# A recurrence and a gated MLP on one core: the order of the operations is read from a stored table instead of planned while building

## The chip, the core and the metric

The kernel runs on one NeuronCore of a Trainium2 chip. The metric is device microseconds of one execution; the time of a kernel is the median over its runs.

Five engines are named as in the profile: PE multiplies matrices, DVE does elementwise and scan work, ACT evaluates functions and copies out of PSUM, POOL does masks and some elementwise work, SP issues all of this kernel's DMAs. Each engine works through its own list of instructions strictly in the order in which the program was built. An instruction whose inputs or buffers are not ready holds up everything behind it on its engine.

## The reference

Per batch and head (4 x 8) a 40x40 state is carried over 768 tokens; the 32 outputs of a token are then joined to a row of 320 numbers, which goes through an MLP without a nonlinearity other than one product.

```python
for t in range(S):                                   # S = 768
    y[:, :, t] = einsum('bhd,bhde->bhe', r[t], state)
    Sa = einsum('bhde,bhe->bhd', state, a[t])
    state = state * w[t][:, :, None, :] - einsum('bhd,bhe->bhde', Sa, b[t]) + einsum('bhd,bhe->bhde', v[t], k[t])
x = y.transpose(0, 2, 1, 3).reshape(B * S, H * D)    # 3072 x 320
out = ((x @ w1) * (x @ w2) @ w3) @ w_out             # d_ff = 1024
```

## The kernel before

The 768 tokens are cut into 12 chunks of 64, and the 32 heads into 2 groups of 8 pairs. What is serial inside a chunk becomes matrix work, and only the state goes from chunk to chunk. For chunk `c` and group `g`:

- `load` fetches the gates and keys (`fm`) and the `a` vectors (`lh`) by SP.
- `scale` makes running products of the gates by a scan on DVE (L436, L441), their inverses on ACT (L445, L448) and DVE (L457, L461), and scales `lh` (L453) and the keys in `fm` (L465), each on DVE or POOL by the chunk.
- `causal` multiplies them on PE (L490); ACT copies the result to `JP` and back to `lh`, POOL masks it (L508).
- `solve` inverts the triangular systems of all 16 pairs of a chunk on DVE alone: a transpose of `JP` into `ab` (L522, its first operation), 36 small products and sums, and two transposes into `TDX` (L597, L600). Each step reads what the one ahead of it wrote.
- `join` completes the inverse on PE (L623, L630).
- `pairs` (L667) and `tokens` (L694) prepare operands on PE.
- `rec` is the recurrence: PE (L718, L725, L733, L745, L778) alternates with ACT copies and four masked copies on DVE (L738), then the new state (L771) and the output `y` (L790) on DVE.
- `gather` moves `y` by 12 DMAs (L800), and `mlp` multiplies the 256 tokens of the chunk by the weights: `xs` is split into a high and a low part (ACT L825, DVE L828), 128 matmuls (L842), the product on DVE (L856), its low part on POOL or DVE (L859), and 48 matmuls (L868).

Ahead of the first `mlp` the weights must be read: `weights` brings them as 64-bit numbers in 31 pieces, and `convert` turns each into fp32 by three DVE operations (L333, L337, L341, each reading what the last wrote) and two on ACT. W3 is first multiplied by the output weights on PE (L404, `product`).

None of these functions emits an instruction at once. Each calls `op(engine, cost, due, fn, r=..., w=...)`, which notes an operation with what it reads and writes. The operations that need a buffer of a pool (`slot`; `bank` is PSUM, 6 of them) name it. After all 2970 operations are noted, `Order.place` plans them: from costs, latencies and due times in the table `P` it simulates the engines, picks the next operation of each and a buffer for it, and the operations are emitted in the order of their planned starts. The instructions of each engine are then tied to that order. The semaphore waits follow from what each one reads and writes.

Of the kernel before, what the change touches and what calls it, by code (L numbers as in the profile page):

```python
# [1 line left out]

# [15 lines left out]
B, H, S, D = 4, 8, 768, 40  # L18
# [15 lines left out]
LAT = dict(pe=0.33, act=0.09, dve=0.09, pool=0.1, sp=2.4, nil=0.0)  # L34
# [4 lines left out]
MODE = {"mlp": 0, "128": 0, "c40t": 0, "c64": 1, "c40": 1, "q64": 2, "32": 3}  # L39
DRAIN, LEAD = 0.1, {"mlp": 0.104, "c40t": 0.02, "32": 0.0}  # L40
# [3 lines left out]
         ga=21.36, ml=83.8, kp=5.81, mt=26.61, mg=18.52, sl=0.56, kw=2.39)  # L44

# [3 lines left out]
class Slot:  # L49


    def __init__(self, order, pool):
        self.order, self.pool, self.at, self.left, self.since, self.until = order, pool, None, 0, 0.0, 0.0
        if order.direct:
            self.at = order.turn[pool] = (order.turn.get(pool, -1) + 1) % SLOTS[pool]
# [6 lines left out]
class Order:  # L62
# [33 lines left out]
    def place(self):  # L96
        ops = self.ops
        for o in ops:
            o["users"], o["wait"] = [], len(o["deps"])
        for o in ops:  # L100
            for d in o["deps"]:
                ops[d]["users"].append(o)
        free = {p: dict.fromkeys(range(n), 0.0) for p, n in SLOTS.items()}
        ready = {e: [] for e in LAT}
        clock, last, lock, dma = {**dict.fromkeys(LAT, 0.0), "pool": 8.0, "dve": 4.0, "sp": 1.0}, None, {"dve": 0.0, "pool": 0.0}, 0.0
        for o in ops:
            o["ready"] = 0.0
            if not o["wait"]:
                ready[o["eng"]].append(o)

        def begin(o):

            t, left = max(o["ready"], clock[o["eng"]]), {}
            for s in o["slots"]:
                if s.at is None:
                    n = left[s.pool] = left.get(s.pool, 0) + 1
                    if len(free[s.pool]) < n:
                        return None
                    t = max(t, sorted(free[s.pool].values())[n - 1])
                else:  # L120
                    t = max(t, s.since)
            if o["two"]:
                t = max(t, lock["pool" if o["eng"] == "dve" else "dve"])
            return t

        uses = {p: {o["eng"] for o in ops for s in o["slots"] if s.pool == p} for p in SLOTS}
        placed, cand, spare = [], {}, {}

        def choice(e, starts):
            if not starts:  # L130
                return None
            first = min(t for t, _ in starts)
            if e != "pe":
                return first, min((o for t, o in starts if t <= first + 1e-9), key=lambda o: (o["due"], o["n"]))
            return min(((t, o) for t, o in starts if t <= first + P["sl"]),
                       key=lambda x: (x[1]["due"] - P["kp"] * (MODE[x[1]["kind"]] == MODE.get(last)) + P["kw"] * (x[0] - first), x[1]["n"]))

        while len(placed) < len(ops):
            best = None
            for e in LAT:  # L140
                if e not in cand:

                    starts, short = [], 1e9
                    for o in ready[e]:
                        t = begin(o)
                        if t is not None:
                            starts.append((t, o))
                        elif e == "pe" and any(s.pool == "bank" and s.at is None for s in o["slots"]):
                            short = min(short, o["due"] + P["mg"])
                    some = [x for x in starts if x[1]["due"] < short or not any(s.at is None for s in x[1]["slots"])]  # L150
                    spare[e] = len(some) < len(starts)
                    cand[e] = choice(e, some)
                if cand[e] and (best is None or cand[e][0] < best[0]):
                    best = cand[e]
            if best is None and any(spare.values()):
                e = "pe"
                best = choice(e, [(t, o) for o in ready[e] if (t := begin(o)) is not None])
            if best is None:
                raise ValueError(f"stuck after {len(placed)} of {len(ops)}")
            t, o = best  # L160
            e = o["eng"]
            ready[e].remove(o)
            stale = {e, *(("dve", "pool") if o["two"] else ())}
            cost = o["cost"]
            if e == "pe":
                if MODE[o["kind"]] != MODE.get(last):
                    cost += DRAIN + LEAD.get(o["kind"], 0.05)
                last = o["kind"]
            for s in o["slots"]:
                if s.at is None:  # L170
                    stale |= uses[s.pool]
                    s.at = min(free[s.pool], key=lambda i: (free[s.pool][i], i))
                    s.since = free[s.pool].pop(s.at)
# [924 lines left out]
```

## Time and profile before

| what | value |
|---|---|
| median of 3 runs | 678.53 us (677.45 to 679.85) |
| span of the profiled execution | 676.2 us |
| PE busy | 577.7 us |
| DVE busy | 551.4 us |
| ACT busy | 431.8 us |
| POOL busy | 211.9 us |

The profiled execution is one run of the same program; its span is counted from its first to its last instruction, and the median of the runs is 2.3 us above it. Busy time counts an engine's working instructions; an engine that waits is not busy. A matmul's end is modelled, so matmuls that follow each other closely overlap in the records. In the rows, `<-` names what ended an idle stretch.

### The profile page before, as it was taken

What the parts mean: (1) busy time and instruction counts of PE and PEld (TensorE: products, weight loads), DVE (VectorE), ACT (ScalarE), POOL (GpSimd) and SP (SyncE); (2) the same over time, 40 slices, a digit from 0 to 9 for tenths busy, and PEclk for the clock granted to TensorE, in tenths of its full rate; (3) what the DMA queues carried; (4) which work ended last, traced back from release to release, by engine and by line L of the source; (5) the groups of instructions that cost most, each with busy time, mean ns of one, the idle gap of its engine ahead of it and who ended that gap; (6) DMA issues with size and microseconds to landing.
All of it is one profiled execution on the core that took longest, in us unless ns stands there. A gap on an engine that the chain in (4) does not pass through costs nothing.

```text
span 676.2 us, 22337 instructions
## 1 busy us (share of the span) xinstructions
PE 577.7 (85%) x9458; PEld 515.3 (76%) x9458; DVE 551.4 (82%) x987; ACT 431.8 (64%) x927; POOL 211.9 (31%) x188
## 2 busy tenths in 40 slices
PE   1422996768799999898999989899999989999996
PEld 1321664556788999788989878789888889898996
DVE  7999999999999799798799798898987997914310
ACT  2886756686776865846837849559578477473321
POOL 4462005233521205505206316245044171120011
PEclk9999997978989999899999999999999999999999
DMA  7954564444214234034133143150341431110101
GB/s 187 245 148 139 169 159 126 132 124 92 60 31 105 69 88 102 14 94 104 33 94 79 32 98 74 42 147 16 83 111 38 99 72 32 45 32 12 34 21 24
DMA packets 61090, 57.56 MB, mean 85 GB/s; under 512 B 29560, under 2 KB 52600, under 8 KB 60984
## 3 DMA queue, kind: packets, MB, share of 16 engines
q1 hardware_dynamic: 60984, 56.07, 32.7%
q8 instruction: 76, 1.25, 0.8%
q14 instruction: 30, 0.25, 0.1%
HBM read 47.40 MB, written 3.93 MB: 76 GB/s over the span
## 4 chain that ended last, share of the span: by engine, by line
DVE 47%; PE 32%; ACT 8%; issue 6%; DMA 4%; POOL 1%; DVEq 0%; SPq 0%; POOLq 0%
PE bank L842 14%; DVE tmp L548 9%; DVE xu L738 6%; PE bank L868 5%; DMA fm<-in_fmx_dram 4%; DVE ab L552 3%; DVE mf L337 3%; ACT JP L212 3%; DVE Tp L552 3%; PE bank L745 2%; DVE fm L441 2%; DVE ab L522 2%; PE bank L725 2%; PE bank L490 2%; DVE w3f L341 2%
## 5 line engine op out<-in xcount | busy, mean ns | idle before, releaser
L842 PE MATMUL bank<-xs,W 128*128 128x256 f32 x1536 | 204.8, 289 | 0.7 <-DVE xs L828 0.7
L842 PEld LDWEIGHTS bank<-xs,W 128*128 128x128 f32 x1536 | 190.3, 193 | 5.8 <-DVE xs L828 0.9
L677 POOL TENSOR_SCALAR_AFFINE_SELECT xu<-xu 64x512 f32<-64x512 f32 x48 | 46.0, 958 | 187.9 <-ACT xu L212 172.1
L212 ACT ACTIVATE xu<-bank 64x256 f32<-64x256 f32 (+2 forms) x184 | 72.6, 437 | 39.4 <-PE bank L718 32.2
L859 POOL TENSOR_TENSOR gl<-ga,gh 128x512 fp32r<-128x512 f32 x32 | 41.0, 1283 | 109.8 <-ACT gh L212 109.8
L212 ACT ACTIVATE JP<-bank 32x512 f32<-32x512 f32 x120 | 60.5, 504 | 22.6 <-PE bank L490 20.7
L490 PE MATMUL bank<-lh,fm 40*64 40x64 f32 x1536 | 32.7, 236 | 45.0 <-POOL fm L465 23.3
L738 DVE TENSOR_TENSOR xu<-bank,mask_h 64x416 f32<-64x416 f32 x96 | 56.3, 587 | 14.0 <-PE bank L733 12.0
L490 PEld LDWEIGHTS bank<-lh,fm 40*64 40x64 f32 x1536 | 29.5, 149 | 49.4 <-POOL fm L465 25.9
L508 POOL TENSOR_SCALAR_AFFINE_SELECT lh<-lh 64x512 f32<-64x512 f32 x48 | 41.0, 853 | 76.8 <-ACT lh L212 73.9
L856 DVE TENSOR_TENSOR ga<-bank,ga 128x512 f32<-128x512 f32 x48 | 32.8, 683 | 39.1 <-PE bank L842 30.3
L868 PE MATMUL bank<-W3h,gh 128*128 128x320 f32 x192 | 63.1, 329 | 1.1 <-DVE xu L738 1.1
L868 PE MATMUL bank<-W3l,gh 128*128 128x320 f32 x192 | 59.2, 309 | 0.0
L868 PE MATMUL bank<-W3h,gl 128*128 128x320 f32 x192 | 59.2, 308 | 0.0
L404 PE MATMUL bank<-wof,w3f 128*128 128x320 f32 x128 | 41.7, 479 | 16.7 <-DVE w3f L341 16.7
L745 PE MATMUL bank<-xu,bk 128*40 128x104 f32 (+1 forms) x768 | 47.5, 262 | 5.9 <-DVE xu L738 5.8
L212 ACT ACTIVATE gh<-ga 128x512 fp32r<-128x512 f32 x48 | 30.3, 631 | 34.6 <-DVE ga L856 34.2
L725 PE MATMUL bank<-xu,lh 128*64 128x104 f32 (+2 forms) x768 | 43.4, 266 | 9.5 <-ACT xu L212 5.8
L453 POOL TENSOR_TENSOR lh<-lh,fm 104x1024 f32<-104x1024 f32 x16 | 35.4, 2216 | 48.4 <-DVE fm L441 22.3
L745 PEld LDWEIGHTS bank<-xu,bk 128*40 128x40 f32 (+1 forms) x768 | 37.5, 120 | 14.7 <-DVE xu L738 12.1
L725 PEld LDWEIGHTS bank<-xu,lh 128*64 128x64 f32 (+2 forms) x768 | 37.6, 144 | 14.2 <-ACT xu L212 6.9
L404 PEld LDWEIGHTS bank<-wof,w3f 128*128 128x128 f32 x128 | 25.8, 210 | 28.7 <-issue 14.3
(99 smaller groups left out, 1190.9 us busy)
## 6 DMA issues: line engine op xcount, KB each, us to landing
fm<-in_fmx_dram SPq DMA_DIRECT2D x24, 627.2 KB
raw<-in_w3t_dram SPq DMA_DIRECT2D x16, 512.0 KB
rv<-in_rv_dram SPq DMA_DIRECT2D x48, 160.0 KB
raw<-in_w_dram SPq DMA_DIRECT2D x8, 512.0 KB
lh<-in_fma_dram SPq DMA_DIRECT2D x48, 80.0 KB
xu<-in_vt_dram SPq DMA_DIRECT2D x48, 80.0 KB
out_dram<-o SPq DMA_DIRECT2D x48, 80.0 KB
xr<-y SPq DMA_DIRECT2D x72, 40.0 KB
```

What stands on the lines that cost most here:

```text
L212: act.activation(out_, in_, AF.Copy, scale=scale)
L404: pe.matmul(out=pt.t[:, 0:DM], lhsT=w[:, j], rhs=wof[:, j], start=(j == 0), stop=(j == NJ - 1))
L490: pe.matmul(out=bank(ab)[64 * x:64 * x + 64, p], lhsT=X[r, p, x], rhs=lh.t[r, ab, p], start=True, stop=True)
L508: pool.affine_select(out=lh.t[q, ab], in_=lh.t[q, ab], pattern=[[0, NP], [1, C]], compare_op=ALU.is_gt, fill=0.0, base=0, channel_multipli ...
L548: dve.tensor_tensor(out=scratch(*shape), in0=x().to_broadcast([128, *shape]), in1=y().to_broadcast([128, *shape]), op=ALU.mult)
L677: op("pool", 0.67, due + 2, lambda q=q, ab=ab: pool.affine_select(out=xu.t[q, ab, :, 0:C], in_=xu.t[q, ab, :, 0:C], pattern=[[0, NP], [1, ...
L725: pe.matmul(out=view(hp[h])[64 * ab:64 * ab + 64, u], lhsT=lh.t[k, ab, HP * h + u], rhs=xu.t[k, ab, HP * h + u], start=True, stop=True)
L738: dve.tensor_tensor(out=xu.t[64 * ab:64 * ab + 64, ab, k:NP:2], in0=view(us[ab])[r], in1=mask_h[r].unsqueeze(1).to_broadcast([64, HP, N]), ...
L745: pe.matmul(out=q(r, p), lhsT=bk.t[:, p, r], rhs=xu.t[:, ab, p], start=(c == 0), stop=True, skip_group_check=True)
L842: pe.matmul(out=pt.t[:, TOK * x:TOK * x + TOK], lhsT=WT[k][:, cs], rhs=xs.t[:, z], start=(n == 0), stop=(n == 7))
L859: both(ON["gl"][c % NCH], 1.3, 0.69, t + 1, lambda e, a=a, j=j: e.tensor_tensor(out=gl.t[:, j:j + 2], in0=a.t, in1=gh.t[:, j:j + 2], op=AL ...
L868: pe.matmul(out=pt.t[:, 0:DM], lhsT=l.t[:, j, ts], rhs=W3[r][:, j], start=(j == 0 and n == 0), stop=(j == NJ - 1 and n == 2))
```

## The change

`place` no longer plans. It decodes a string of numbers, `PLAN`: for each place in the program the operation that stands there, and for each buffer wanted the number that it gets. The same 2970 operations are emitted with the same costs and functions; the assertions only check that the order keeps every dependence. Two names, `turn` and `turns`, keep the weight pieces' loads and their first conversion steps in the order of the pieces.

```diff
-LAT = dict(pe=0.33, act=0.09, dve=0.09, pool=0.1, sp=2.4, nil=0.0)
...
+PLAN = """
+c-n<n2XvKH);;IG_tHo}iVluttf+_}NEc1$f+z_fN)-h~K%|!#0;JFhRX|Wj5kyoV1f(UQNdnRtz!4Rc@n;+r0Z9TO<(@P9do3^g|5|_6%6Gr-)^pF@d!K
...
     def place(self):
-        ops = self.ops
+        ops, n = self.ops, len(self.ops)
+        code = array("h", zlib.decompress(base64.b85decode("".join(PLAN.split()))))
+        turns, at = list(accumulate(code[:n])), iter(code[n:])
+        assert sorted(turns) == list(range(n))
         for o in ops:
...
-        while len(placed) < len(ops):
-            best = None
-            for e in LAT:
...
-        self.placed = sorted(placed, key=lambda o: (o["start"], o["n"]))
-        return self.placed
+        done, holder = set(), {}
+        placed = [ops[i] for i in turns]
+        for o in placed:
+            assert o["deps"] <= done
...
+        return placed
...
-        op("sp", 0.35, due - 8, f1, w=[raw], dma=2.5)
+        op("sp", 0.35, due - 8, f1, w=[raw, "turn"], dma=2.5)
...
-        op("dve", 0.42, due, f4, r=[raw], w=[mf], two=True)
+        op("dve", 0.42, due, f4, r=[raw], w=[mf, "turns"], two=True)
```

In the changed file a line of the functions above has a number that is 24 lower (L828 is L804 there). On all engines the order moves; three places are shown.

The first place is DVE near its start, where the first two pieces of the weights (`raw_139`, `raw_140`) are converted. Before:

```order
L333 TENSOR_SCALAR mf_145<-raw_139 128x512
L337 SCALAR_TENSOR_TENSOR mf_145<-raw_139,mf_145 128x512
L341 SCALAR_TENSOR_TENSOR mf_145<-raw_139,mf_145 128x512
L453 TENSOR_TENSOR lh_98<-lh_98,fm_94 104x1024
L333 TENSOR_SCALAR mf_146<-raw_140 128x512
L337 SCALAR_TENSOR_TENSOR mf_146<-raw_140,mf_146 128x512
L341 SCALAR_TENSOR_TENSOR mf_146<-raw_140,mf_146 128x512
```

Of the change, the same two pieces:

```order
L309 TENSOR_SCALAR mf_145<-raw_139 128x512
L441 TENSOR_TENSOR fm_93<-fm_93,gi_100 104x1024
L313 SCALAR_TENSOR_TENSOR mf_145<-raw_139,mf_145 128x512
L309 TENSOR_SCALAR mf_146<-raw_140 128x512
L317 SCALAR_TENSOR_TENSOR mf_145<-raw_139,mf_145 128x512
L313 SCALAR_TENSOR_TENSOR mf_146<-raw_140,mf_146 128x512
L417 SCALAR_TENSOR_TENSOR fm_95<-fm_95,first 104x520
L317 SCALAR_TENSOR_TENSOR mf_146<-raw_140,mf_146 128x512
```

The three steps of a piece stood next to each other, each reading the one ahead; now another piece or another chunk's scaling stands between them.

The second place is DVE just ahead of the first `mlp`, whose low part `xs` is written by L828 (`xu_106`, `st_110`, `y_111` from `fm_95` belong to `rec` of chunk 1, group 1; `fm_94` here to `scale` of chunk 3; `ab` to the solve of chunk 2). Before:

```order
L436 TENSOR_SCALAR fm_94,stats<-fm_94 104x520
L738 TENSOR_TENSOR xu_106<-bank_131,mask_h 64x4x104
L738 TENSOR_TENSOR xu_106<-bank_130,mask_h 64x4x104
...
L548 TENSOR_TENSOR tmp<-Tp,ab 128x512
L552 TENSOR_REDUCE ab<-tmp 128x16x4
L771 TENSOR_TENSOR st_110<-bank_134,fm_95 104x160
L790 TENSOR_TENSOR y_111<-bank_134,fm_95 104x4x64
...
L441 SCALAR_TENSOR_TENSOR fm_94<-fm_94,first 104x520
L453 TENSOR_TENSOR lh_98<-lh_98,fm_94 104x1024
L828 TENSOR_TENSOR xs_1519<-xr_112,xs_1519 128x768
```

Of the change:

```order
L524 TENSOR_TENSOR tmp<-Tp,ab 128x1024
L747 TENSOR_TENSOR st_110<-bank_131,fm_94 104x160
L766 TENSOR_TENSOR y_111<-bank_131,fm_94 104x4x64
L528 TENSOR_REDUCE ab<-tmp 128x16x4
L747 TENSOR_TENSOR st_110<-bank_134,fm_94 104x160
L766 TENSOR_TENSOR y_111<-bank_134,fm_94 104x4x64
L804 TENSOR_TENSOR xs_1410<-xr_112,xs_1410 128x768
L524 TENSOR_TENSOR tmp<-ab,DG 128x512
L528 TENSOR_REDUCE Tp<-tmp 128x8x8
```

The eight DVE operations of chunk 1, group 1 and three of chunk 3's scaling now stand behind the first `xs`; two long steps of the solve of chunk 2 stand ahead of it.

The third place is DVE where the solve of chunk 8 begins with the transpose of `JP_113` (`fm_93` is chunk 8's second group). Before:

```order
L457 TENSOR_TENSOR gt_101<-fm_93,gi_100 104x512
L461 SCALAR_TENSOR_TENSOR gi_100<-gt_101,gi_100 104x512
L465 TENSOR_TENSOR fm_93<-fm_93,gi_100 104x1024
L856 TENSOR_TENSOR ga_1520<-bank_134,ga_1520 128x512
L522 STREAM_TRANSPOSE ab<-JP_113 128x1024
```

Of the change:

```order
L441 TENSOR_TENSOR fm_93<-fm_93,gi_100 104x1024
L528 TENSOR_REDUCE R_128<-tmp 128x8x8
L568 TENSOR_TENSOR ab<-R_128,ab 128x8x8
L524 TENSOR_TENSOR tmp<-ab,DG 128x512
L528 TENSOR_REDUCE Tp<-tmp 128x8x8
L573 STREAM_TRANSPOSE TDX_102<-Tp 128x32x16
L576 STREAM_TRANSPOSE TDX_102<-TDX_102 128x512
L498 STREAM_TRANSPOSE ab<-JP_113 128x1024
```

Between the scaling of the keys and the transpose stood one operation of 128x512; now the last six steps of the solve of chunk 7 stand there.

## Rows read from the trace of the kernel before

**Rows 1.** The page: span, busy time, 40 slices, engines of the chain.

```profile
span 676.2 us, 22337 instructions
...
PE 577.7 (85%) x9458; PEld 515.3 (76%) x9458; DVE 551.4 (82%) x987; ACT 431.8 (64%) x927; POOL 211.9 (31%) x188
...
PE   1422996768799999898999989899999989999996
...
DVE  7999999999999799798799798898987997914310
...
DVE 47%; PE 32%; ACT 8%; issue 6%; DMA 4%; POOL 1%; DVEq 0%; SPq 0%; POOLq 0%
```

**Rows 2.** Windows: us, busy us of five engines, PE clock, DMA share, GB/s.

```profile
0.00:170.54 170.54, 100.61 (x1489) 75.66 (x1489) 158.98 (x287) 116.37 (x277) 58.93 (x62) 0.94 0.57 152
170.54:670.00 499.46, 476.95 (x7969) 439.69 (x7969) 392.31 (x699) 314.96 (x651) 152.95 (x126) 0.99 0.26 63
670.00:676.20 6.20, 0.10 (x2) 0.00 (x0) 0.15 (x1) 0.44 (x1) 0.00 (x0) 0.79 0.20 39
```

**Rows 3.** Timeline of DVE ahead of the first MLP: start, us, instruction.

```profile
161.28 0.70 DVE L436 TENSOR_SCALAR_CACHE_REDUCE fm<-fm 104x520 f32<-104x520 f32 x1 [0.26 <-DMA fm<-in_fmx_dram]
...
164.38 0.69 DVE L548 TENSOR_TENSOR tmp<-Tp,ab 128x512 f32<-128x512 f32 x1
165.10 0.69 DVE L552 TENSOR_REDUCE ab<-tmp 128x64 f32<-128x512 f32 x1
...
167.13 1.23 DVE L441 TENSOR_TENSOR_SCAN fm<-fm,first 104x520 f32<-104x520 f32 x1
168.39 1.23 DVE L453 TENSOR_TENSOR lh<-lh,fm 104x1024 f32<-104x1024 f32 x1
169.53 0.95 DVE L828 TENSOR_TENSOR xs<-xr,xs 128x768 fp32r<-128x768 f32 x1
```

**Rows 4.** Timeline of PE, same place.

```profile
170.54 1.68 PE L842 MATMUL bank<-xs,W 128*128 128x256 f32 x12 [0.70 <-DVE xs L828]
```

**Rows 5.** Who DVE waited for, 10 to 170 us: total, times, longest.

```profile
DVE fm L436 <- DMA fm<-in_fmx_dram: 1.9, 3, 1.4
```

**Rows 6.** Groups by line and shape: busy, mean ns.

```profile
L552 DVE TENSOR_REDUCE ab<-tmp 128x64 f32<-128x1024 f32 x12 | 14.7, 1222 | 0.2
L548 DVE TENSOR_TENSOR tmp<-Tp,ab 128x1024 f32<-128x1024 f32 x12 | 14.6, 1218 | 0.3
```

**Rows 7.** Window, 157.55 to 169.48 us.

```profile
157.55:169.48 11.93, 9.98 (x153) 7.88 (x153) 11.10 (x21) 9.46 (x21) 6.37 (x6) 0.86 0.44 95
```

**Rows 8.** Who PE waited for, from the first MLP matmul on.

```profile
PE bank L490 <- POOL fm L465: 6.7, 4, 2.7
PE bank L623 <- DVE TDX L600: 2.1, 2, 1.1
...
PE bank L490 <- issue: 1.9, 3, 1.4
```

**Rows 9.** Who DVE waited for, 170.6 to 592 us.

```profile
DVE ab L522 <- ACT JP L212: 23.4, 8, 3.9
```

**Rows 10.** Timeline of DVE, start of the solve of chunk 8.

```profile
419.27 2.19 DVE L465 TENSOR_TENSOR fm<-fm,gi 104x1024 f32<-104x1024 f32 x1
...
424.97 2.02 DVE L522 STREAM_TRANSPOSE ab<-JP 128x1024 f32<-128x1024 f32 x1 [2.54 <-ACT JP L212]
```

**Rows 11.** Timeline of SP, the first loads.

```profile
0.82 0.46 SPq L424 DMA_DIRECT2D fm<-in_fmx_dram  x1
2.04 0.66 SPq L427 DMA_DIRECT2D lh<-in_fma_dram  x2
```

**Rows 12.** Window, the first 25 us.

```profile
0.00:25.00 25.00, 7.13 (x144) 6.31 (x144) 20.61 (x27) 11.03 (x23) 11.75 (x25) 1.00 0.84 213
```

**Rows 13.** Timeline of DVE, end of the last solve.

```profile
592.84 0.71 DVE L600 STREAM_TRANSPOSE TDX<-TDX 128x512 f32<-128x512 f32 x1
```

**Rows 14.** Timeline of PE, the last join.

```profile
596.31 1.20 PE L623 MATMUL bank<-TDX,JP 32*32 32x32 f32 x64
```

More of the change, by code (lines that the diff above doesn't have):

```diff
@@ L1 @@
+import base64
+import zlib
+from array import array
 from contextlib import ExitStack
+from itertools import accumulate
 import concourse.bass as bass
@@ L46 @@
+4&uh+w~m4*VM07+{MH&jzADe{4&o}*s(`Jo;4a*iuoJ2mo)BDfkd5vj0xSH>!PNu4GJY0NCA53|^SOf_b5-&Y2QePXxC(?+oFMu4XZ${Mg(!n3hy!=XUVJ
+C$4q*@nacV+V@C5Dk1UXn4e^g1ODt7D%u_~Y~uAomU&ZGj{fwe;QDm0Ez5EmvGS6nwmql!~=hj6Dd+R5)D<JVPpCA&Ge6BFXY0LI*vG%?^6Pe{ZF*yr+d{
+AT+q6sSVOTtN=HLOg0hkngU9O;_+#Js~Ru)XB$qSCBpb1^6}XS^
+"""
 ON = dict(ws="p", lh="pdpddppdpppp", xs="dpppdpdpdddp", gl="pdpdppppdpdp")
@@ L52, in __init__ @@
     def __init__(self, order, pool):
-        self.order, self.pool, self.at, self.left, self.since, self.until = order, pool, None, 0, 0.0, 0.0
+        self.order, self.pool, self.at, self.left = order, pool, None, 0
         if order.direct:
@@ L96, in place @@
     def place(self):
-        ops = self.ops
+        ops, n = self.ops, len(self.ops)
+        code = array("h", zlib.decompress(base64.b85decode("".join(PLAN.split()))))
+        turns, at = list(accumulate(code[:n])), iter(code[n:])
+        assert sorted(turns) == list(range(n))
         for o in ops:
[L99 to L113, printed above, removed]
             for s in o["slots"]:
                 if s.at is None:
[L116 to L136, printed above, removed]
@@ L138, in place @@
-        while len(placed) < len(ops):
-            best = None
-            for e in LAT:
[L141 to L168, printed above, removed]
-            for s in o["slots"]:
[L170 to L173, printed above, removed]
-            clock[e] = t + cost
-            if o["two"]:
-                lock[e] = clock[e]
-            done = clock[e] + LAT[e]
-            if e == "sp":
-                dma = max(dma, clock[e]) + o["dma"]
-                done = dma + LAT[e]
-            o["start"], o["end"] = t, clock[e]
-            placed.append(o)
-            for s in o["slots"]:
-                s.until, s.left = max(s.until, done), s.left - 1
-                if not s.left:
-                    stale |= uses[s.pool]
-                    free[s.pool][s.at] = s.until
-            for u in o["users"]:
-                u["wait"] -= 1
-                u["ready"] = max(u["ready"], clock[e] if u["eng"] == e != "sp" else done)
-                if not u["wait"]:
-                    stale.add(u["eng"])
-                    ready[u["eng"]].append(u)
-            for e in stale:
-                cand.pop(e, None)
@@ L196, in place @@
-        self.placed = sorted(placed, key=lambda o: (o["start"], o["n"]))
-        return self.placed
+                    s.at = next(at)
+                    assert 0 <= s.at < SLOTS[s.pool]
+        done, holder = set(), {}
+        placed = [ops[i] for i in turns]
+        for o in placed:
+            assert o["deps"] <= done
+            done.add(o["n"])
+            for s in o["slots"]:
+                h = holder.get((s.pool, s.at))
+                assert h is s or h is None
+                s.left -= 1
+                holder[s.pool, s.at] = s if s.left else None
```

52 lines of the change are left out of this document (50 added, 2 removed).

## The prediction, made before the changed kernel ran

> **What bounds the kernel now.** I read the page first, then windows cut where the work changes, then the waits on the two busy engines, then their timelines. PE and DVE are both busy for over 80% of the span, and the chain that ended last goes through both, DVE 47% and PE 32% [rows 1]. That is an average over stages with different limits, which the slices show: DVE's digits stand at 9 in the first quarter while PE's start at 1; at the end PE stands at 9 and DVE falls to 1. The windows put the border at 170.54 us, where the first stretch of MLP matmuls that runs on begins [rows 2, 4]. Up to there DVE is busy 159.0 of 170.5 us and PE only 100.6. From there to the last matmul at 670.0 PE is busy 476.95 of 499.46 us, so it is idle for 22.5. The last 6.2 us are copies, stores and the final check.
>
> So two limits follow each other. In the first part DVE waits for almost nothing: after its start, 1.9 us for loads of `fm` is its largest item [rows 5]. The MLP can't begin before all weights are converted and `xs` is split, and all of that stands in DVE's list: the matmuls wait for L828, which starts at 169.53 and takes 0.95 [rows 3, 4]. In the second part PE carries the time. The span is therefore the time of the first L828, plus PE's work behind it, plus PE's idle time behind it, plus 6.2. I work out each of these four for the new order.
>
> **What the change does, part by part.** No operation is added or removed, so only places in the lists, buffers and waits can move the time.
>
> *DVE's neighbours.* In rows 3, L453 reads what L441 wrote, and starts 0.03 us behind its end (167.13 + 1.23 = 168.36, start 168.39). L828 reads nothing of L453, and starts 0.09 us ahead of its end (168.39 + 1.23 = 169.62, start 169.53). That holds widely: over the trace, 471 neighbours on DVE of which the second reads or overwrites what the first wrote lie a median of 0.034 us apart, and 436 that are free of each other overlap by a median of 0.082. So a neighbour that depends costs 0.116 us more. I counted such neighbours in both lists. Ahead of the first L828 there are 144 before and 43 now, as the braided conversions of the first place show; up to the end of the last solve there are 473 and 307. The first count gives 101 x 0.116 = 11.7 us less ahead of the first MLP, the second 19.3 us up to the last solve. Between L738's neighbours the trace shows no overlap (95 pairs, 0.03 apart); counting those apart changes the sum by 0.1. The bounds are 0, if other neighbours don't overlap as these do, and 13.
>
> On this point the Trainium skill (VectorE: DVE Perf Modes, section "The DRAIN you can't avoid") says that after every DVE operation the pipeline must empty before the next starts, that chaining cannot skip it, and that one should reduce the number of operations. By that rule this term would be 0. The overlap of L453 and L828 speaks against it, and so does the section "Two Vector instructions with no wait between them" of the same page, by which only a held instruction must wait for all earlier ones to finish.
>
> *Work moved behind the first L828.* The second place shows it. Four L738, two L771, two L790 of chunk 1 and L436, L441, L453 of chunk 3 leave the stretch from 161.28 to 169.53, which holds besides them only two solve steps of 0.69 and 0.2 of waiting [rows 3]: 8.25 - 1.4 - 0.2 = 6.7 us. Two solve steps of 1.22 each come in [rows 6]. Net 4.3 us less.
>
> *The start.* SP now issues two loads of `lh` (80 KB each) ahead of the first `fm`, and these wait for a memset of their buffer; before, the first `fm` went out at 0.82 and `lh` at 2.04 [rows 11]. At 213 GB/s [rows 12] 160 KB are 0.75 us. I take 0.7 later; the bounds are 0 and 1.6.
>
> *New waits of DVE in the first part.* If DVE gets ahead by 12 us, its feeders must keep up. Before it waited little [rows 5]; ACT was busy 116 and POOL 59 of 170 us [rows 2], so there is room. I take 1.0, between 0 and 6.
>
> The first L828 then ends at 170.5 - 11.7 - 4.3 + 0.7 + 1.0 = 156.2 us.
>
> *PE's work behind it.* Twelve PE operations (`rec` of chunk 1, group 1, `tokens` and `pairs` of chunk 2) that stood ahead of the first MLP now stand behind. They filled 157.55 to 169.48, where PE was busy 9.98 us at a granted clock of 0.86 [rows 7]. At full clock that is at most 0.86 x 9.98 = 8.6, and some of it is waiting between modelled ends, so 8, between 6 and 10. I counted PE's changes between kinds of matmul also: 276 before, 275 now, so nothing there. Work behind: 477 + 8 = 485.
>
> *PE's idle time behind it.* The waits that make up the 22.5 us name DVE or POOL for 15.2 us (most of it L490 waiting for the scaled keys, 6.7, and L623 for the solve, 2.1), ACT for 5.1 and nothing for 1.9 [rows 8]. Two things shrink the first part. DVE arrives earlier at everything by the 0.116 us. And DVE itself waits 23.4 us, eight times, for `JP` at the start of a solve [rows 9], because the keys' scaling, `causal` on PE and ACT's copies must follow each other while DVE has almost nothing to do. For chunk 8 it is 2.54 us behind one operation [rows 10]; the third place puts six steps of the last solve there (4.1 us of work), more than that wait. For chunks 7 to 11 such cover grows by about 2 us each, for 4 and 6 hardly, for 5 it falls by 1.7. Taking each cover from its wait leaves about 13 of 23.4 us. I leave the 7 us that name ACT or nothing, and 4 of the 15.2: the list has PE reach the join of chunk 4 sixteen operations sooner, so the solve of that chunk is needed sooner. Idle 11, between 4 and 22.5.
>
> *Does DVE become the limit again?* The last solve ends at 592.84 + 0.71 [rows 13]. Less 19.3 and about 10 it ends near 564. The join behind it starts at 596.31 [rows 14] and 73.7 us of PE follow before 670.0; there are now 8 PE operations fewer behind it, so about 66. 564 + 3 + 66 + 6 = 639, below the sum that follows. PE stays the limit.
>
> **Sum.** 156.2 + 485 + 11 + 6.2 = 658.4 us of span, against 676.2. The median of the runs lies 2.3 above that execution's span, so 660.7; I say 660.5.
>
> **Rivals.** *The early start is kept, the idle time too.* Waits only move to other places: idle 22.5, span 669.9, time 672. For it speaks that half of PE's waits come from chains over three engines; against it, that the solves have more cover.
>
> *PE hardly waits.* DVE runs far ahead, idle 4: span 651.4, time 653.7. Against it: ACT's waits don't depend on DVE's order.
>
> *The order saves nothing on DVE, and the time rises.* Place: DVE ahead of the first L828. If neighbours in the new list cost what dependent ones cost now, L828 ends at 156.2 + 11.7 = 167.9, the idle time stays at 22.5, and 8 us of PE work have moved behind the start: 167.9 + 485 + 22.5 + 6.2 = 681.6, time 683.9, slower. The Trainium skill's rule on the DRAIN, named above, would give this case. The order turns to a loss where the saving per neighbour falls below 0.054 us (5.4 of 11.7 us, with the idle time as before). Against it stand 436 overlapping neighbours.
>
> **How the numbers follow.** The forecast (654 to 668) has 0.55, the kept idle time (668 to 675) 0.22, PE hardly waiting (below 654) 0.11, no saving (above 676) 0.08; 0.04 lies between. The range of 8 in 10 goes from 648, all terms at their good bounds (153 + 483 + 4 + 6 + 2.3), to 675, the forecast with the idle time of before and some of DVE's new waits. A measurement tells 0.3% from no change, 2 us. Faster by more than that 0.88, within it 0.04, slower 0.08.
>
> **What would show it.** Right: the first long stretch of L818 (the L842 of now) begins near 156 us; DVE's busy time up to there falls by about 16 us; the waits of L498 for `JP` sum to about 13; PE's idle time from there on is near 11. Wrong: neighbours that don't overlap; DVE waiting for loads or ACT ahead of 156 us; or new PE waits on L599 and L466 in the middle chunks that give the early start back.

## The result, and the profile after

The changed kernel takes 671.91 us (median of 4 runs, 671.01 to 673.22) against 677.99 for the kernel before beside it: a ratio of 0.9906, 95% interval 0.9879 to 0.9933. It ran once more beside some of the experiments:

> The changed kernel itself, unaltered, to have its time on the same chip as the kernels beside it. Expected as measured before: 0.9906 of the kernel before, about 671.9 us.

There it came out at 673.8 us, a ratio of 0.9926 (0.9898 to 0.9953). It is faster, but by 5 to 6 us where the forecast said 18. Of the ways that were foreseen it is nearest to the first rival, the early start kept and the idle time too.

The page of the changed kernel, the lines that answer to [rows 1]:

```profile
span 671.0 us, 22253 instructions
...
PE 570.0 (85%) x9458; PEld 510.4 (76%) x9458; DVE 532.5 (79%) x987; ACT 421.9 (63%) x927; POOL 203.5 (30%) x188
...
PE 43%; DVE 33%; DMA 9%; ACT 7%; issue 5%; POOL 2%; SPq 0%; DVEq 0%; ACTq 0%; POOLq 0%
```

DVE is busy 19 us less, and the chain leans on PE more than on DVE. The DMAs have more of it, 9% of the span against 4%; the loads of `fm` alone have 8%, and had 4%. The windows are cut as [rows 2] was, at the first L818 that starts behind the end of `xs`, and at the last matmul of the MLP:

```profile
0.00:162.58 162.58, 89.39 (x1338) 68.42 (x1338) 147.62 (x278) 106.77 (x261) 58.64 (x60) 0.93 0.52 149
162.58:662.98 500.40, 480.45 (x8119) 441.93 (x8119) 384.70 (x709) 314.71 (x666) 144.86 (x128) 1.00 0.27 66
662.98:671.00 8.02, 0.19 (x2) 0.09 (x2) 0.15 (x1) 0.44 (x1) 0.00 (x0) 0.66 0.12 31
```

The four parts of the sum can be read off: 162.58 us to the first L818, PE busy 480.45 behind it and idle for 500.40 - 480.45 = 19.95, and 8.02 at the end. The timelines at the border, DVE first and PE under it, answer to [rows 3, 4]:

```profile
158.66 1.22 DVE L528 TENSOR_REDUCE ab<-tmp 128x64 f32<-128x1024 f32 x1
...
161.56 0.96 DVE L804 TENSOR_TENSOR xs<-xr,xs 128x768 fp32r<-128x768 f32 x1 [1.14 <-ACT xs L801]
```

```profile
162.19 1.50 PE L818 MATMUL bank<-xs,W 128*128 128x256 f32 x8
```

L804 now has to wait: DVE stands 1.14 us for ACT's half of the split, where it stood for nothing before. It is one of several new waits ahead of the first MLP. The list of DVE's waits from 8 to 162.58 us answers to [rows 5] (total, times, longest; 1.9 us of the wait for `fm` lie ahead of the first scaling):

```profile
DVE fm L412 <- DMA fm<-in_fmx_dram: 4.8, 3, 2.3
DVE W3l L385 <- ACT W3h L188: 1.6, 1, 1.6
DVE xu L714 <- PE bank L709: 1.1, 1, 1.1
DVE xs L804 <- ACT xs L801: 1.1, 1, 1.1
DVE y L766 <- PE bank L721: 1.1, 1, 1.1
DVE ab L498 <- ACT JP L188: 0.8, 1, 0.8
DVE stats L994 <- ACT sq L306: 0.6, 1, 0.6
```

The same view from 162 to 592 us answers to [rows 9]. The wait for `JP` at the start of a solve has nearly gone, from 23.4 to 5.2 us. In its place DVE stands 16.7 us for loads of `fm`, where the kernel before had 5.9 in five, and 15.3 us for PE's own products (`ga`), where it had 1.4:

```profile
DVE fm L412 <- DMA fm<-in_fmx_dram: 16.7, 8, 6.7
DVE ga L832 <- PE bank L818: 15.3, 9, 4.7
DVE ab L498 <- ACT JP L188: 5.2, 7, 1.6
```

And PE's waits from 162.5 to 663 us, which answer to [rows 8]. The 6.7 us for scaled keys are down to 0.9; what is left are many small waits for copies that the recurrence itself orders from DVE and ACT. Over the whole view, DVE or POOL is named for 8.9 us (15.2 before), ACT for 7.6 (5.1) and nothing for 2.4 (1.9):

```profile
PE bank L721 <- DVE xu L714: 3.5, 7, 1.5
PE bank L754 <- DVE st L747: 3.0, 9, 0.6
PE bank L701 <- ACT xu L188: 1.9, 2, 1.5
...
PE bank L709 <- ACT hs L188: 1.4, 3, 0.6
...
PE bank L466 <- POOL fm L441: 0.9, 3, 0.4
```

The time up to the end of `xs` can be split exactly along DVE's list, since DVE works through it in order: the start of the first L412 (L436 before), the durations of the operations up to `xs`, the gaps below 0.3 us between neighbours (negative where they overlap), and the gaps of 0.3 us or more, which are waits. I summed these over DVE's rows of each trace, in us (accumulator reads and the two small operations on `stats` count as gaps):

| kernel | first scaling starts | durations | small gaps | waits | end of `xs` |
|---|---|---|---|---|---|
| before | 7.38 | 162.0 | -1.7 | 2.8 | 170.5 |
| changed | 9.34 | 157.4 | -13.6 | 9.3 | 162.5 |
| unbraid | 9.08 | 162.9 | -2.8 | 9.1 | 178.2 |
| before_braided | 7.38 | 162.0 | -14.0 | 17.1 | 172.5 |
| before_braided_mf3 | 7.37 | 161.3 | -14.4 | 16.7 | 171.0 |

### The profile page after: what moved, and what is told of

Its sections match the earlier page's. It is cut to its first block, busy times and chain, and to the rows that moved or that the text cites. A ratio compares the mean times of both kernels' runs of the same rounds, so it can differ in the third digit from the quotient of the medians.

```text
span 671.0 us, 22253 instructions
## 1 busy us (share of the span) xinstructions
PE 570.0 (85%) x9458; PEld 510.4 (76%) x9458; DVE 532.5 (79%) x987; ACT 421.9 (63%) x927; POOL 203.5 (30%) x188
## 4 chain that ended last, share of the span: by engine, by line
PE 43%; DVE 33%; DMA 9%; ACT 7%; issue 5%; POOL 2%; SPq 0%; DVEq 0%; ACTq 0%; POOLq 0%
PE bank L818 18%; DMA fm<-in_fmx_dram 8%; PE bank L844 7%; DVE tmp L524 6%; DVE xu L714 4%; PE bank L466 3%; PE bank L721 3%; DVE ab L528 3%; PE bank L701 2%; ACT JP L188 2%; DVE mf L313 2%; POOL fm L441 2%; PE bank L754 2%; DVE DG L528 1%; DVE Tp L528 1%
## 5 line engine op out<-in xcount | busy, mean ns | idle before, releaser
L818 PE MATMUL bank<-xs,W 128*128 128x256 f32 x1536 | 202.2, 286 | 2.7 <-ACT ga L188 1.5
L818 PEld LDWEIGHTS bank<-xs,W 128*128 128x128 f32 x1536 | 187.0, 189 | 7.8 <-ACT ga L188 1.7
L653 POOL TENSOR_SCALAR_AFFINE_SELECT xu<-xu 64x512 f32<-64x512 f32 x48 | 36.3, 761 | 180.8 <-ACT xu L188 179.6
L188 ACT ACTIVATE xu<-bank 64x256 f32<-64x256 f32 (+2 forms) x184 | 72.4, 436 | 29.6 <-PE bank L694 15.7
L835 POOL TENSOR_TENSOR gl<-ga,gh 128x512 fp32r<-128x512 f32 x32 | 43.9, 1372 | 106.9 <-ACT gh L188 106.7
L188 ACT ACTIVATE JP<-bank 32x512 f32<-32x512 f32 (+1 forms) x120 | 59.7, 501 | 12.9 <-PE bank L466 11.1
L484 POOL TENSOR_SCALAR_AFFINE_SELECT lh<-lh 64x512 f32<-64x512 f32 x48 | 38.0, 791 | 63.4 <-ACT lh L188 63.0
L701 PE MATMUL bank<-xu,lh 128*64 128x104 f32 (+2 forms) x768 | 44.4, 270 | 14.5 <-ACT xu L188 10.7
L701 PEld LDWEIGHTS bank<-xu,lh 128*64 128x64 f32 (+2 forms) x768 | 39.0, 147 | 19.3 <-ACT xu L188 12.2
L188 ACT ACTIVATE ga<-bank 128x512 f32<-128x512 f32 x48 | 28.6, 596 | 31.6 <-PE bank L818 30.8
L380 PE MATMUL bank<-wof,w3f 128*128 128x320 f32 x128 | 39.6, 462 | 4.1 <-DVE w3f L317 4.1
```

The lines of the kernel that those rows point to most:

```text
L188: act.activation(out_, in_, AF.Copy, scale=scale)
L380: pe.matmul(out=pt.t[:, 0:DM], lhsT=w[:, j], rhs=wof[:, j], start=(j == 0), stop=(j == NJ - 1))
L484: pool.affine_select(out=lh.t[q, ab], in_=lh.t[q, ab], pattern=[[0, NP], [1, C]], compare_op=ALU.is_gt, fill=0.0, base=0, channel_multipli ...
L653: op("pool", 0.67, due + 2, lambda q=q, ab=ab: pool.affine_select(out=xu.t[q, ab, :, 0:C], in_=xu.t[q, ab, :, 0:C], pattern=[[0, NP], [1, ...
L701: pe.matmul(out=view(hp[h])[64 * ab:64 * ab + 64, u], lhsT=lh.t[k, ab, HP * h + u], rhs=xu.t[k, ab, HP * h + u], start=True, stop=True)
L818: pe.matmul(out=pt.t[:, TOK * x:TOK * x + TOK], lhsT=WT[k][:, cs], rhs=xs.t[:, z], start=(n == 0), stop=(n == 7))
```

## The experiments

Theory after the result: the neighbours on DVE save what was forecast; but a faster DVE runs into its feeders, ahead of the first MLP and, through the loads of `fm`, behind it. Rivals: neighbours cost the same in any order, and the gain is from elsewhere; or PE's idle time is made by the recurrence's own copies, whatever the loads do. Every ratio is to the kernel before, run beside it. In the traces of kernels whose order was written anew, lines are a few numbers higher; the text names them by the changed kernel's.

### The braid taken out, and put in alone

`unbraid` is the changed kernel with each piece's three steps side by side again on DVE:

```diff
  L437 gi<-gt,gi
+ L441 fm<-fm,gi
  L309 mf<-raw       (piece 0)
- L441 fm<-fm,gi
  L313 mf<-raw,mf    (piece 0)
+ L317 mf<-raw,mf    (piece 0)
+ L417 fm<-fm,first
  L309 mf<-raw       (piece 1)
- L317 mf<-raw,mf    (piece 0)
  L313 mf<-raw,mf    (piece 1)
- L417 fm<-fm,first
  L317 mf<-raw,mf    (piece 1)
```

> The changed kernel, with the three conversion steps of each of the 31 weight pieces standing next to each other again on DVE (each at the place of its third step); nothing else moves. Dependent neighbours ahead of the first L818 rise from 43 to 132. Theory 'neighbours': 89 x 0.116 = 10.3 us, the first long stretch of L818 begins near 172.5 instead of 162.2, and the time rises to about 682. Rival 'the order saves nothing on DVE' (neighbours cost the same wherever they stand): L818 at 162, time 672. Rival 'feeders': DVE's waits ahead of the first MLP, about 15 us in all, shrink when DVE is slower, L818 near 167, time near 677.

Measured: 689.12 us, ratio 1.0172 (1.0147 to 1.0197). The table gives 10.7 us more in small gaps, against 10.3 expected: the order of neighbours alone is worth that. The waits stayed (9.3 and 9.1), so the feeders gave nothing back. The rule of the Trainium skill that was weighed in the prediction (VectorE: DVE Perf Modes, "The DRAIN you can't avoid") would, taken for every operation, have left this kernel at 672, and falls for this case; the section itself points to operations that are not held and start earlier. But `xs` came 15.7 us later, not 10.7: the durations rose by 5.5 too. The groups of the second conversion step ahead of the first MLP, of `unbraid` and then of the changed kernel, show where:

```profile
L322 DVE SCALAR_TENSOR_TENSOR mf<-raw,mf 128x512 uint32<-128x512 uint32 x31 | 28.2, 909 | 1.1
```

```profile
L313 DVE SCALAR_TENSOR_TENSOR mf<-raw,mf 128x512 uint32<-128x512 uint32 x31 | 21.3, 686 | 0.0
```

909 against 686 ns for the same instruction. Of the 31 in `unbraid`, 20 that lay beside no POOL instruction took a mean of 0.69 us and none over 0.70, and 11 that overlapped one took 1.30 (the longest 3.33). The changed kernel has such company too, at the first step: its 31 take a mean of 557 ns, one of them 3.20 us beside two POOL instructions, against 428 ns in `unbraid`. The three steps together are 5.3 us longer in `unbraid`, so nearly all of the 5.5 is not the neighbours but the company on POOL, and an order has that in its hands as well. Behind the first MLP `unbraid` also has 486.5 us of PE's work, 6.1 more; that was not followed.

`before_braided` is the one part alone: the kernel before, in which only DVE's list ahead of the first MLP is braided.

```diff
  L457 gt<-fm,gi
+ L441 fm<-fm,first
  L461 gi<-gt,gi
+ L333 mf<-raw       (piece 0)
  L465 fm<-fm,gi
- L441 fm<-fm,first
- L333 mf<-raw       (piece 0)
  L337 mf<-raw,mf    (piece 0)
+ L333 mf<-raw       (piece 1)
  L341 mf<-raw,mf    (piece 0)
```

> The kernel before's own order and buffers, in which only DVE's list ahead of the first MLP is changed: an operation that is free of its neighbour is pulled between two that depend, at most two places away, so that dependent neighbours fall from 144 to 29. No other engine's list changes, nor DVE's behind the first MLP. Theory 'neighbours': 115 x 0.116 = 13.3 us, the first long stretch of L842 begins near 157.2 instead of 170.5, PE's idle time behind it stays near 22, and the time falls to about 665, below the changed kernel's 671.9. Rival 'feeders': loads of weights, ACT and PE cannot follow a faster DVE, DVE's waits grow, L842 near 163 to 165, time near 671. Rival 'not kept': L842 at 157 but PE waits 10 us more behind it, time near 675.

Measured: 679.85 us, ratio 1.0047 (1.0022 to 1.0072). The small gaps shrank by 12.3 us, about as expected, and every bit of it went into waits, which grew from 2.8 to 17.1. DVE's waits from 8 to 172.5 us:

```profile
DVE mf L313 <- POOL W L362: 4.2, 1, 4.2
DVE gt L437 <- ACT gi L428: 3.6, 3, 1.9
DVE fm L416 <- DMA fm<-in_fmx_dram: 3.6, 3, 1.3
DVE W3l L389 <- ACT W3h L192: 3.4, 3, 1.3
```

An order in which DVE never waits is not one in which DVE is the only limit. Its feeders were planned to be just in time. Does one of them bind, or all?

```diff
-             raw=4, sq=2, mf=2, w3f=2, xs=1, gh=1, gl=1, ga=2, o=2)
+             raw=4, sq=2, mf=3, w3f=2, xs=1, gh=1, gl=1, ga=2, o=2)
```

> The braided order on the kernel before, with three buffers mf instead of two; the order is the same. In the braided kernel DVE's waits ahead of the first MLP grew from 2.8 to 17.1 us and ate the 12.3 us that the neighbours saved; 4.2 of the growth were waits for POOL to have read mf, 3.8 for ACT's gi, 3.4 for ACT's W3h. Theory 'feeders, one by one': the 4 us for mf go, the others stay or grow, the first long stretch of L842 begins near 168 to 170 (172.6 braided, 170.5 before), time 3 to 4 us under the braided kernel's 1.0047 of before, about 0.999. Rival 'the buffers bind': all waits go, L842 near 160, time near 0.985 of before. Rival 'the next feeder takes it': no change, 1.0047.

Measured: 678.49 us, ratio 1.0025 (1.0005 to 1.0045). The wait for `mf` is gone and the others took its place; DVE's waits from 8 to 172 us:

```profile
DVE gt L438 <- ACT gi L429: 5.5, 5, 2.6
DVE W3l L390 <- ACT W3h L193: 4.9, 5, 2.0
DVE fm L417 <- DMA fm<-in_fmx_dram: 4.7, 3, 1.7
```

17.1 us of waits became 16.7, and ACT is named for most of them. But ACT's own list is late in only about half of these. In the others ACT stood idle itself, once until DVE had read the single buffer `gi`, and three times until PE's product for W3 was there; two of the four places, on ACT:

```profile
17.64 0.63 ACT L426 ACTIVATE gi<-fm 104x512 f32<-104x512 f32 x1 [6.82 <-DVE fm L446]
72.66 0.44 ACT L193 ACTIVATE W3h<-bank 128x320 fp32r<-128x320 f32 x1 [2.50 <-PE bank L385]
```

So what isn't ready for a faster DVE is a list in some places, and in others a chain over two engines or a buffer that DVE itself still holds. The 1.5 us by which `xs` came earlier are 0.2% of the time; the intervals of the two kernels overlap.

### The start

`fm_first` puts the loads of chunk 0's `fm` back at the head of SP's list:

```diff
         turns, at = list(accumulate(code[:n])), iter(code[n:])
+        for i in (249, 246):
+            turns.remove(i)
+            turns.insert(0, i)
```

> The changed kernel, with the loads of chunk 0's two fm put back at the head of SP's list, ahead of lh. Theory 'the start passes through': in the changed kernel DVE's first L412 began at 9.34 us (7.38 before) and its first three waits for fm were 1.9, 2.3 and 0.5 us; with fm first DVE begins near 7.4, and the first long stretch of L818 comes 2 to 3 us earlier, near 159.5 instead of 162.2. PE's idle time behind it stays at 20, so the time falls by 2 to 3 us, to about 669.5. Rival 'the early start is not kept': the waits behind take it back, L818 begins earlier but the time stays at 671.9.

In the changed kernel, SP's first loads, which answer to [rows 11], were these:

```profile
2.04 1.36 SPq L403 DMA_DIRECT2D lh<-in_fma_dram  x2
3.44 0.33 SPq L400 DMA_DIRECT2D fm<-in_fmx_dram  x1
```

With `fm` first, DVE's first scaling starts at 7.37 in place of 9.34, and PE's stretch of MLP matmuls at 160.20 in place of 162.19: the 2 us pass through in full, and the span is 668.6 instead of 671.0. The time, 670.68 us and 0.9913 of before (0.9892 to 0.9933), can't be told from the changed kernel's 0.9906 and 0.9926. So the trace shows the term and the time doesn't resolve it. A second trace of the changed kernel has `xs` ready at 161.54 instead of 162.52, so a single trace gives such a term to about 1 us.

### The loads of fm behind the first MLP

In the changed kernel each load of `fm` from chunk 2 on goes out within 1.8 us of the last read of its buffer, and the first L412 that needs it starts 5.6 to 8.0 us after the issue. `split_load` leaves the order alone, and only lets the part come first that is needed first:

```diff
-        op("sp", 0.4, due, lambda: sp.dma_start(out=fm.t, in_=fmx[c, g]), w=[(fm, "g"), (fm, "x")], dma=3.0)
+        def both_parts():
+            n = NP * W65
+            sp.dma_start(out=fm.t[:, 0:n], in_=fmx[c, g, :, 0:n])
+            sp.dma_start(out=fm.t[:, n:], in_=fmx[c, g, :, n:])
+
+        op("sp", 0.4, due, both_parts, w=[(fm, "g"), (fm, "x")], dma=3.0)
```

> The changed kernel, with each load of fm issued as two DMAs, the gates' 520 columns first and the keys' 1024 behind; DVE's L412 needs the gates alone. In the changed kernel DVE waited 16.7 us behind the first MLP for loads of fm that are issued when the buffer comes free and take 6 to 7 us. Theory 'late loads': DVE's waits for fm fall to about 5 us, PE's idle time behind the first MLP falls from 20 to about 14, and the start gains 1 to 2 us, time about 665. Rival 'the recurrence's own copies': PE's waits are for L714, L747 and ACT's copies that stand behind other work in DVE's and ACT's lists; DVE's waits for fm fall, PE's idle time stays at 20, and only the start's 1 to 2 us come through, time about 670.

Measured: 664.11 us, ratio 0.9806 (0.9789 to 0.9824): 1.0 to 1.2% below the changed kernel's 0.9906 and 0.9926, and the fastest of this study. Its windows, and DVE's waits from 162 to 592 us:

```profile
0.00:160.77 160.77, 89.89 (x1336) 68.62 (x1336) 149.96 (x279) 106.96 (x261) 58.59 (x60) 0.91 0.52 151
160.77:656.06 495.29, 479.07 (x8124) 441.60 (x8120) 384.40 (x708) 314.76 (x665) 145.67 (x128) 1.00 0.27 67
656.06:662.80 6.74, 0.19 (x2) 0.09 (x2) 0.14 (x1) 0.44 (x1) 0.00 (x0) 0.66 0.14 36
```

```profile
DVE fm L417 <- DMA fm<-in_fmx_dram: 5.8, 2, 4.1
```

DVE's waits for `fm` fell from 16.7 to 5.8 us, and PE's idle time from 19.95 to 495.29 - 479.07 = 16.22. The span's 8.2 us are 1.8 at the start, 1.4 of PE's work (two traces of the changed kernel differ by 3.0 in it), 3.7 of idle time and 1.3 at the end. So late loads are a part of the idle time that was kept, not all of it. The same edit on the kernel before:

> The kernel before, with each load of fm issued as two DMAs, gates first, and no other change. Theory 'the new order made the loads matter': in the kernel before DVE waited only 5.9 us for loads of fm behind the first MLP against 16.7 in the changed one, so the split brings the start's 1 us and 1 to 2 behind, time about 675 to 676. Rival 'the split helps any order': 8 us less, as it gave the changed kernel, time near 669.

Measured: 676.75 us, ratio 0.9961 (0.9933 to 0.9989). The edit is worth 0.4% there and 1.0 to 1.2% in the new order. That is what the loads had taken: with both kernels' loads split, the change of order is worth 1 - 0.9806 / 0.9961 = 1.6%, some 10.5 us, and not 5 to 6.

### The waits of the recurrence

`rec_first` moves 66 of the recurrence's operations up in DVE's list, past solve steps, outputs `y` and scaling that ran while their input was already there; one place of 66:

```diff
  L714 xu<-bank,mask_h
- L528 ab<-tmp         (solve of chunk 6)
  L714 xu<-bank,mask_h
  L714 xu<-bank,mask_h
  L714 xu<-bank,mask_h
+ L528 ab<-tmp         (solve of chunk 6)
  L524 tmp<-Tp,ab      (solve of chunk 6)
```

> The changed kernel, with 66 operations of the recurrence on DVE behind the first MLP (L714, L747) moved up in DVE's list, past steps of a solve or of the scaling that ran ahead of them while, by the changed kernel's trace, their own input was already there. Nothing else moves. In the changed kernel PE waited 19.95 us behind the first MLP, 3.5 of it for L714 (xu) and 3.0 for L747 (st). Theory 'behind other work': the order puts solve steps ahead of the recurrence's copies, so PE waits for these; with the copies first the idle time falls by 5 to 8 us, time about 666. Rival 'covered anyway': PE then waits for the solve, the loads or ACT in its place, idle stays near 20, time 671 to 673. Rival 'solve late': the solve steps pushed back come too late for the join, idle over 22, time over 674.

Measured: 683.15 us, ratio 1.0059 (1.0033 to 1.0084), slower than both kernels. PE's idle time rose to 26.6 us. Its waits from 162.3 us on:

```profile
PE bank L764 <- DVE st L757: 7.2, 6, 3.2
PE bank L828 <- DVE ga L842: 2.5, 2, 1.6
PE bank L609 <- DVE TDX L586: 2.2, 4, 1.0
...
PE bank L731 <- DVE xu L724: 1.1, 3, 0.7
```

The wait that was aimed at did shrink (3.5 to 1.1 for `xu`); those for `st`, `ga` and `TDX` grew by more. My theory, that the copies only stood behind work that could wait, falls: the work pushed behind them was needed as soon. In the longest of the new waits (3.2 us) DVE's `st` stands behind a `gt` that waits 0.7 us for ACT's `gi` and takes 1.4 itself. A smaller cut of the same kind, on top of `split_load`: 19 of the `st` ahead of the `y` in front of them.

```diff
  L747 st<-bank,fm
+ L747 st<-bank,fm
  L766 y<-bank,fm
  L766 y<-bank,fm
- L747 st<-bank,fm
```

> The changed kernel with the split loads of fm, and on DVE 19 of the 44 L747 (the state, for which PE's L754 waits) moved ahead of the L766 (the output y, for which nothing waits soon) directly in front of them; 0.41 us each. Theory 'behind y': PE's waits for st, 3.4 us in 9 in the kernel with split loads, fall to about 1, time 1 to 3 us less, near 662. Rival 'moved on': as with the recurrence's copies moved up, the waits come back in other places, time 664 or more.

Measured: 664.31 us, ratio 0.9817 (0.9787 to 0.9848): no difference from `split_load`. PE's waits for `st` fell from 3.4 to 1.9 us and its idle time from 16.2 to 15.9. The first theory here is wrong in size, and the rival, that waits move on, fits.

### The cover of the solves

`uncover` puts the last solve steps of a chunk ahead of the last three scaling operations of the next one again, at four places; chunk 8:

```diff
- L433 gt<-fm,gi        (chunk 8)
  L528 ab<-tmp          (solve of chunk 7)
...
- L437 gi<-gt,gi        (chunk 8)
...
- L441 fm<-fm,gi        (chunk 8)
...
  L576 TDX<-TDX         (solve of chunk 7)
+ L433 gt<-fm,gi        (chunk 8)
+ L437 gi<-gt,gi        (chunk 8)
+ L441 fm<-fm,gi        (chunk 8)
  L498 ab<-JP           (solve of chunk 8)
```

> The changed kernel, in which the last steps of the solve ahead of the start of the next one (29 operations, 20.3 us, in chunks 4, 6, 8 and 10) stand ahead of the last three scaling operations of the new chunk again, and not between these and the transpose of JP. Theory 'cover': DVE then waits for JP again with nothing to do, 2 to 4 us at each of four places, its waits for JP rise from 5.2 to about 15 us, and the scaled keys reach PE 2 to 5 us later at each place; PE's idle time rises by 4 to 8 us, time near 677 to 680. Rival 'slack': DVE waits for JP, but PE has other work and its idle time stays near 20, time within 2 us of the changed kernel.

Measured: 694.99 us, ratio 1.0273 (1.0237 to 1.0308), 3.5 to 3.7% (some 24 us) over the changed kernel. DVE's waits from 162.2 to 620 us, PE's from 162 to 685, and the window between the first L818 and the last matmul:

```profile
DVE ab L509 <- ACT JP L199: 20.9, 9, 6.5
```

```profile
PE bank L477 <- issue: 16.9, 4, 5.0
```

```profile
162.23:685.15 522.92, 488.33 (x8119) 449.90 (x8119) 387.46 (x709) 314.53 (x666) 144.01 (x128) 0.97 0.26 63
```

The waits for `JP` are back at 20.9 us. PE stands four times, 3.4 to 5.0 us each, ahead of `causal`. The profile names no releaser there, but each time `causal` starts 0.1 to 0.2 us behind the end of DVE's scaling of the keys:

```profile
427.31 1.23 DVE L452 TENSOR_TENSOR fm<-fm,gi 104x1024 f32<-104x1024 f32 x1
428.64 0.65 PE L477 MATMUL bank<-lh,fm 40*64 40x64 f32 x13 [4.99 <-issue]
```

PE's idle time is 522.92 - 488.33 = 34.6, so 14.6 more, and its work behind the first L818 takes 7.9 us more at a clock of 0.97 instead of 1.00. Windows around one of the four waits show where that comes from:

```profile
410.00:423.50 13.50, 13.50 (x138) 13.38 (x127) 12.97 (x22) 7.70 (x16) 5.39 (x5) 1.00 0.27 63
423.50:428.60 5.10, 0.15 (x2) 0.00 (x0) 4.93 (x7) 1.43 (x3) 1.18 (x1) 0.76 0.00 0
428.60:432.00 3.40, 3.36 (x71) 3.28 (x71) 0.00 (x0) 1.31 (x3) 1.20 (x2) 0.50 0.00 0
432.00:436.00 4.00, 4.00 (x84) 3.83 (x84) 0.92 (x1) 3.06 (x7) 0.51 (x1) 0.88 0.00 0
```

The seventh number is the granted clock. PE is busy at 1.00 (2.4 GHz), stands idle for 5 us while DVE works, and then does 3.4 us of matmuls at 0.50 (1.2 GHz) before the clock comes back. That loses 3.4 x 0.50 + 4.0 x 0.12 = 2.2 us on top of the wait. The other three places, read alike, lose 1.7 to 3.4, and the four together 9.6, where PE's work took 7.9 more in all. The whole is the largest single effect in the study, and three to four times the 5 to 8 us that I expected. It is the price of the cover in a list of PE that counts on it, and not what the change gained by it: in the kernel before, whose list didn't count on it, PE's waits for scaled keys were 6.7 us.

### The early part of the order, alone

`early_part_only` takes the changed order up to its first MLP matmul, and the order of before for all that is left.

> The changed order for every operation that stands ahead of its first MLP, and the kernel before's order for all that is left; buffers as in either, but for 8 of 1003 that had to be chosen anew. Theory 'the early part carries the gain': the idle time and the tail behind are those of before (22.5 and 6.2 us), 162.6 + 480.5 + 22.5 + 6.2 = 671.8 us of span, time near 673. Rival 'the later part carries it': the early start is lost in waits of the old order, idle time near 28, time near 678.

Measured: 687.03 us, ratio 1.0122 (1.0072 to 1.0172). Neither theory: idle time (22.0) and end (6.1) are those of before, but the early start is lost ahead of the MLP. DVE at `xs`, then PE at the first MLP matmuls, and the window between:

```profile
161.40 0.96 DVE L807 TENSOR_TENSOR xs<-xr,xs 128x768 fp32r<-128x768 f32 x1 [1.14 <-ACT xs L804]
```

```profile
176.77 0.48 PE L821 MATMUL bank<-xs,W 128*128 128x256 f32 x2
```

```profile
162.35:176.77 14.42, 9.94 (x152) 7.71 (x151) 6.72 (x14) 5.60 (x15) 1.31 (x2) 0.88 0.49 101
```

`xs` is ready at 162.4, but PE's list holds the twelve operations of chunks 1 and 2 first, as in [rows 7], and they take until 176.77. An early `xs` is worth nothing unless PE's list has the MLP next; the change moved both. The experiment does not split the gain, as it was meant to.

## Why the prediction was wrong, step by step

The forecast was a span of 658.4 and the changed kernel's is 671.0, 12.6 us more. By the four terms of the sum:

| term | forecast | measured | difference |
|---|---|---|---|
| first L818 | 156.2 | 162.58 | +6.4 |
| PE's work behind | 485 | 480.45 | -4.55 |
| PE's idle time behind | 11 | 19.95 | +8.95 |
| end | 6.2 | 8.02 | +1.8 |

*Neighbours: right ahead of the first MLP.* 11.7 us forecast, 13.6 - 1.7 = 11.9 in the small gaps, and 10.7 the other way in `unbraid`. Behind it, from the first `xs` to the end of the last solve, the forecast's count gave 19.3 - 11.7 = 7.6 us; there the small gaps shrank by only 2.4 (-4.7 to -7.1). The 0.034 and -0.082 us of the kernel before hold in all traces. That the busy time would fall by 16 was a slip of the text: the gaps between dependent neighbours are not busy time; it fell by 11.4.

*Moved work: right.* 4.3 forecast, 4.6 in the durations.

*The start: too small.* 0.7 forecast, with bounds 0 and 1.6; 9.34 - 7.38 = 1.96 measured. I priced the bytes of the two `lh`, not the wait for the memset that holds up SP's whole list: the first `fm` goes out at 3.44 instead of 0.82. `fm_first` gives the 2 us back in the trace.

*New waits of DVE: the step that failed ahead of the MLP.* 1.0 forecast, 9.3 - 2.8 = 6.5 measured, just past my bound of 6. Of the 9.3 us, some 4.2 name ACT, 2.9 loads of `fm` and 2.2 PE; none names POOL. I took ACT's and POOL's busy shares as a sign that they had room. Busy time doesn't tell when an engine's list gets to the one operation that is wanted. `before_braided` shows the same more clearly: with the feeders' lists unchanged, all of a saving of 12.3 us turned into waits, and with one buffer more other feeders took it.

*PE's work: too large in this trace.* 8 us added by the forecast, 3.5 measured. A second execution of the changed kernel had 483.43 in place of 480.45, so 6.5 added, which is inside my bounds of 6 to 10: this term is known to some 3 us only.

*PE's idle time: the step that failed behind the MLP, and the largest.* I reckoned that DVE's earlier arrival would take 11 of the 15.2 us that named DVE or POOL and leave the 7 that named ACT or nothing; 8.9 and 10.0 were left, and a second execution had 21.07 us of idle time in place of 19.95. The cover itself was right and stronger than forecast: waits for `JP` fell to 5.2, not 13, the wait for scaled keys went from 6.7 to 0.9, and `uncover` shows that with the cover undone at four places the time rises by some 24 us. What I missed is what is late next. A DVE that gets to a chunk's scaling sooner stands for the load of `fm`, which can't leave sooner: it goes out when the recurrence two chunks back lets go of the buffer. I had priced DVE's waits for `JP` and left its waits for loads as they were. `split_load` takes 10.9 us of these waits away, and PE's idle time falls by 3.7. Of the other 5.2 us the runs show what they are (waits of up to 1.5 us, for `xu`, `st`, `hs` above all) and that two ways of moving DVE's operations don't remove them; whether another order would, stays open.

*The end: too small by 1.8.* The copies and stores of the last tokens are the same; the check of the weights on PE stands behind the last copy of ACT now, 0.5 us after the last MLP matmul, where it stood 0.1 ahead of that matmul's end. `split_load`, with the same order there, ends after 6.74 us, so the check is not all of it; the rest stays open.

*Rivals.* The first, that waits only move, gave 672 and a chance of 0.22; it named the outcome within 0.1 us, though partly by chance, since early start and end were off too. That DVE's order saves nothing is excluded by `unbraid`.

*DVE as the limit: not as forecast.* I had the last solve end near 564, which left PE the limit by some 19 us. It ended at 595.91 (593.55 before), and its join on PE began 0.47 us later:

```profile
595.20 0.71 DVE L576 STREAM_TRANSPOSE TDX<-TDX 128x512 f32<-128x512 f32 x1
596.38 1.20 PE L599 MATMUL bank<-TDX,JP 32*32 32x32 f32 x64
```

From the first `xs` to that solve I had DVE's waits fall by about 10 us; summed as in the table, they rose from 37.7 to 53.2. What the cover gave went into waits for loads and for PE's own products. So DVE has no lead: in every chunk the join starts within 1.6 us of its solve's end, where the kernel before had up to 10.9 between them, and the chain that ended last runs through DVE's steps of the last solve from 569.7 to 591.4 us. PE was not idle just ahead of that join, so DVE is not shown to be the limit there either.

## What to carry to other kernels

Where an engine that never waits is made faster, price its feeders before the gain is written down: for each input, when it can leave at the earliest (a buffer that comes free, a list that gets there, a chain that starts at the faster engine itself), not how busy its engine is. Where a wait is covered, ask what the covered engine reaches sooner, and what that needs. A load that goes out when its buffer is freed can still be cut so that the part needed first lands first: that was worth about as much as the whole new order to which it was added (1.0 to 1.2% against 0.7 to 0.9%), and 0.4% without it.

## What the runs showed of the hardware

- DVE operations that don't depend on the one ahead start before it ends: a median of 0.08 us of overlap, against a gap of 0.034 for dependent ones, the same in all seven kernels in which I looked.
- The same DVE instruction on 128x512 elements took 0.69 us alone and 1.30 on average beside a POOL instruction, up to 3.33; not each such meeting costs this, for six that met one in the changed kernel took a mean of 0.71. The Trainium skill (SBUF — State Buffer, "SBUF: two separate sides") says that GpSimd and a DVE operation with two SBUF inputs, as this one has, contend for a pair of ports that whoever starts first holds for a whole instruction while the other is blocked; the lengthening agrees with that, and by it an order should keep long POOL instructions away from such DVE work.
- Behind each of four waits of PE of 3.4 to 5.0 us in `uncover` the granted clock stood at 0.50 to 0.53 for the next 3 us and more of matmuls. PE's work took 7.9 us longer in all, half of the 14.6 us that the idle time grew by; some 3 us of such a difference can be the spread between executions.
- A load of 627 KB cut into 211 and 416 KB (520 and 1024 of 1544 columns, with 24 more DMAs in all) let DVE start sooner at no cost that the trace shows (the DMA share behind the first MLP is 0.27 in both).
